# Start of an attention backward kernel reordered, 32 matmuls put ahead of it, and all wq and wo loads tied to program order two ticks earlier

## The chip, the cores and the metric

The kernel runs on one core of one Trainium2 chip. A core has a matrix engine (PE, whose weight loads are listed apart as PEld), a vector engine (DVE), a scalar engine (ACT), a GpSimd engine (POOL) and a sync engine (SP). The engines run side by side, each through its own list of instructions in order, and wait for each other through semaphores. Transfers are issued by SP and by POOL in this kernel and are carried out by 16 DMA engines that both share. The metric is the device time of one execution in microseconds (us), as the median of several runs.

## The reference

Two independent attention blocks, A and B, are computed forward and backward. For each block

```python
q = (x @ wq).reshape(B, Sq, H, Dh).transpose(0, 2, 1, 3)
scores = einsum("bhqd,bhkd->bhqk", q, k_cache) * Dh ** -0.5
p = softmax(scores)
o = einsum("bhqk,bhkd->bhqd", p, v_cache)
out = o.transpose(0, 2, 1, 3).reshape(B, Sq, H * Dh) @ wo
```

with B = 8 batches, Sq = 96 queries, D = 640, H = 32 heads, Sk = 512 keys and Dh = 128, all in bfloat16. The two outputs are concatenated. Results are this output and, for a given `grad_out`, the gradients of x, k_cache, v_cache, wq and wo of both blocks. So each of the 2 x 32 x 8 = 512 pairs of a head and a batch needs the scores, the softmax P, the output O, and backward dV = P^T dO, dP = dO V^T, dS = P (dP - row sum of O dO), dK = dS^T Q and dQ = dS K; around these stand the projections of each head (Q = x wq, dO = g wo^T) and the weight gradients (dwo = O^T g, dwq = x^T dQ).

## The kernel before, in words

The program is written as many small closures. Each is entered in a list with a tick and a slot (`Emitter.add`), the list is sorted by tick, then slot, and the closures are called in that order. One tick is one pair of a head and a batch; head h of a block begins at `c0t = tick0 + 8 h`, and block B follows block A without a pause. The table `OFF` says how many ticks after its own tick a stage of a pair runs: the scores S and the exponential at +3, the normalised P at +3, the transpose of P and dV at +4, O at +5, dP and dS at +6, dK at +7, dQ at +8. So one tick holds stages of several pairs, and the matrix engine's list interleaves them.

The table `HK` does the same for the work of a whole head: `pA` (line 172) loads wo of the head and, on even heads, wq of two heads; `pB` (line 186) transposes both on PE; `pC` (line 207) computes QT (which = 0) and dOT (which = 1), each in a piece of 512 and one of 256 columns; `pD` (line 227) transposes them to dOnat and Qnat; `qA`, `qB`, `qD` make dwo and dwq. After the last head of a group of five or six heads, `gU` (line 488) sums the group's part of the output and of dx, spread over the following ticks.

For one pair: SP loads K and V of two batches at a time. K is transposed either on PE (`c_s1`, line 260, with the copy KT_pe by DVE) or by a DMA transpose, V always by a DMA transpose VT (`c_xt`). PE makes S (line 278); DVE takes the negative row maximum `negm` (280); ACT makes the exponential E_sb (290); DVE takes the reciprocal `rinv` (300); POOL multiplies to P_sb (309); PE transposes P (332) and makes dV (349), O (325), dP (377), and so on. POOL also multiplies O by dO (`prod`, 367), and it issues the stores of dV and dK (358), the stores of dwo (461), dwq (483) and the first block's output (513), and all loads of wo and wq (179, 180) but the first wq.

The tile framework places instructions on each engine's list by its own planning, which may differ from the order of the calls; an instruction that has gone through `keep_in_program_order` (`pinned`, line 107) keeps its place between the neighbours that it was written with. In the kernel before, `pA` of block A pins the loads of heads 1 to 8, and the rest are placed by the planner. wo_h has nine buffers, wq_p two. A buffer of wo_h comes free when `gU` of its group has read it.

The start of block A: SP's first transfers are the first four sixths of x, wq of heads 0 and 1, the rest of x, K, g (the block's half of grad_out, in two parts), V, and more K and V. PE transposes x (six pieces of five 128x128 transposes, `setup_T`, line 118), each piece copied to xT by DVE, then wo and wq of head 0, then g, each piece copied to gT by ACT; then come QT, dOT, dOnat, Qnat and the first scores. For block B the same x and g pieces are loaded into `ld_tmp` by POOL (line 114) and transposed during the last ticks of block A.

Of the kernel before, what the change touches and what calls it, by code (L numbers as in the profile page):

```python
# [10 lines left out]
F32 = mybir.dt.float32  # L11
BF16 = mybir.dt.bfloat16
# [28 lines left out]
SL_HEAD = 90  # L41
SL_GRP = 95
SL_SETUP = 96

OFF = dict(ldk=-5, ldv=-3, kt=-1, vt=2, s2=3, s3=3, s4=4, s5=5, s6=6, s7=7, s8=8)
HK = dict(pA=-7, pB=-3, pC0=[-2, 0], pC1=[-1, 0], pD1=1, pD0=2, qA0=13, qA1=17, qB=[20, 17], qD=[(18, 0, 2), (19, 2, 4), (20, 4, 5)])
EV = dict(pB0="act", pB1="dve", pC00="act", pC01="act", pC10="act", pC11="dve", pD0="dve", pD1="dve", qA0="dve", qA1="dve", qB0="act", qB1="act", qD="dve", gU="act")
GSPREAD0 = 9
PRIO_OFF = 2000
# [4 lines left out]
def build_block(tc, em, tick0, blk, x, kc, vc, wq, wo, g_all, out_all, dx, dk, dv, dwq, dwo, ident, ones, pools, HG=6, first=True, groups=None):  # L54
    nc = tc.nc
    B, Sq, D = x.shape
    _, H, Sk, Dh = kc.shape
# [6 lines left out]
    NB = 2  # L64
    assert B % NB == 0 and H % 2 == 0
    scale = float(Dh) ** -0.5
    HG = min(HG, H)
# [26 lines left out]
    const, ps, kvp, wk, hd, hst, grp = (pools[k] for k in ("const", "ps", "kvp", "wk", "hd", "hst", "grp"))  # L94

    def bank(shape, dt, name):
        return ps.tile(shape, dt, name=name, tag="bank")
# [20 lines left out]
    def setup_T(which_, t):  # L118
        def f():
            key = "xT" if which_ == 0 else "gT"  # L120
            if t == 0:
                S[key] = const.tile([128, DC, T], BF16, name=key, bufs=1)
            dst = S[key]
            if first:
                tmp = S["x_nat" if which_ == 0 else "g_nat"][:, t, :]
            else:
                tmp = S.pop(("tmp", which_, t))
            pt = bank([128, DC * 128], BF16, "tp_ps")
            for c in range(DC):
                nc.tensor.transpose(pt[:, c * 128:(c + 1) * 128], tmp[:, c * 128:(c + 1) * 128], ident[:])  # L130
            evac("act" if first and which_ == 1 else "dve", dst[:, :, t * 128:(t + 1) * 128], pt[:].rearrange("p (c k) -> p c k", k=128))
        return f

    def setup_nat(which_):
# [20 lines left out]
    def evac(eng, dst, src, sc=None):  # L155
        if eng == "act":
            nc.scalar.activation(dst, src, ACT.Identity, scale=(1.0 if sc is None else sc))
        else:
            if sc is None:
                nc.vector.tensor_copy(dst, src)  # L160
            else:
                nc.vector.tensor_scalar(dst, src, float(sc), None, op0=ALU.mult)

    xg = [(0, t) for t in range(min(4, TT))] + [(1, t) for t in range(min(4, TT))] + [(w, t) for w in (0, 1) for t in range(4, TT)]
    for i, (which_, t) in enumerate(xg):
        if not first:
            em.add(tick0 - 12 + i // 2, SL_LOAD, setup_ld(which_, t))
        em.add(tick0 + ((-8 if which_ == 0 else -3) if first else -8 + i // 2), SL_SETUP, setup_T(which_, t))
    em.add(tick0 + (-11 if first else B + OFF["s5"] - 2), SL_LOAD + 1, setup_nat(1))
    em.add(tick0 + (-12 if first else B + OFF["s8"] - 2), SL_LOAD, setup_nat(0))  # L170

    def pA(h):
        def f():
            wo_h = hst.tile([128, D], BF16, name="wo_h", bufs=HG + 3)
            order = pinned if first and 0 < h < HG + 3 else (lambda ins: ins)
            if h % 2 == 0:
                wq_p = hd.tile([128, DC, 256], BF16, name="wq_p", bufs=2)
                with nc.allow_non_contiguous_dma(reason="wq slice of two heads"):
                    order((nc.sync if first and h == 0 else nc.gpsimd).dma_start(wq_p[:], wq_v[:, :, h * 128:(h + 2) * 128]))
            order(nc.gpsimd.dma_start(wo_h[:], wo[h * 128:(h + 1) * 128, :]))  # L180
            if h % 2 == 1:
                wq_p = HS[(blk, h - 1)]["wq_p"]
            HS[(blk, h)] = dict(wo_h=wo_h, wq_p=wq_p, wq_h=wq_p[:, :, (h % 2) * 128:(h % 2 + 1) * 128])
        return f
# [329 lines left out]
        return f  # L514

    NTS = len(tsplits)
    S45 = pools["S45"]
    S78 = pools["S78"]
    for g in range(NG):
        h0 = GH0[g]  # L520
        for hh in range(groups[g]):
            h = h0 + hh
            c0t = tick0 + h * B
            if not (first and h == 0):
                em.add(c0t + HK["pA"], SL_LOAD, pA(h))
            em.add(c0t + HK["pB"], SL_HEAD, pB(h))
            for si in range(NTS):
                em.add(c0t + HK["pC0"][min(si, len(HK["pC0"]) - 1)], SL_HEAD, pC(h, 0, si))
                em.add(c0t + HK["pC1"][min(si, len(HK["pC1"]) - 1)], SL_HEAD, pC(h, 1, si))
            em.add(c0t + HK["pD1"], SL_HEAD, pD(h, 1))  # L530
            em.add(c0t + HK["pD0"], SL_HEAD, pD(h, 0))
            for b in range(B):
                ct = c0t + b
                if b % NB == 0:
                    em.add(tick0 - 12 if first and h == 0 and b == 0 else ct + OFF["ldk"], SLOTS["LOAD"], c_ld(h, b, "K", 7))
                    em.add(ct + OFF["ldv"], SLOTS["LOAD"], c_ld(h, b, "V", 5))
                    if (b // NB) % 2 == 1:
                        em.add(ct + OFF["kt"], SLOTS["LOAD"] + 1, c_xt(h, b, "KT", 2))
                    em.add(ct + OFF["vt"], SLOTS["LOAD"] + 1, c_xt(h, b, "VT", 3))
                if (b // NB) % 2 == 0:  # L540
                    em.add(ct + 2, SLOTS["S1"], c_s1(h, b))
                em.add(ct + OFF["s2"], SLOTS["S2A"], c_s2a(h, b))
                em.add(ct + OFF["s2"], SLOTS["S2B"], c_s2b(h, b))
                em.add(ct + OFF["s3"], SLOTS["S3A"], c_s3a(h, b))
                em.add(ct + OFF["s3"], SLOTS["S3B"], c_s3b(h, b))
                em.add(ct + OFF["s5"], SLOTS["S5B"], c_s5b(h, b))
                if b % 2 == 1:
                    em.add(ct + OFF["s4"] + 1, SLOTS["LOAD"], c_st(h, b, "v"))
                    em.add(ct + OFF["s7"] + 1, SLOTS["LOAD"], c_st(h, b, "k"))
                em.add(ct + OFF["s4"], SLOTS["S4"], c_s4(h, b))  # L550
                S45.setdefault(ct + OFF["s5"], [None, None, None])[0] = (blk, h, b)
                S45.setdefault(ct + OFF["s4"], [None, None, None])[1] = (blk, h, b)
                S45.setdefault(ct + OFF["s6"], [None, None, None])[2] = (blk, h, b)
                S78.setdefault(ct + OFF["s8"], [None, None])[0] = (blk, h, b)
                S78.setdefault(ct + OFF["s7"], [None, None])[1] = (blk, h, b)
                em.add(ct + OFF["s6"], SLOTS["S6"], c_s6(h, b))
                em.add(ct + OFF["s7"], SLOTS["S7"], c_s7(h, b))
            em.add(c0t + HK["qA0"], SL_HEAD, qA(h, 0))
            for di in range(len(dsplits)):
                em.add(c0t + HK["qB"][min(di, len(HK["qB"]) - 1)], SL_HEAD + 1, qB(h, di))  # L560
            em.add(c0t + HK["qA1"], SL_HEAD, qA(h, 1))
            qd_parts = HK["qD"]
            for (k_, c_lo, c_hi) in qd_parts:
                if c_lo < DC and h % 2 == 1:
                    em.add(c0t + k_, SL_HEAD + 2, qD(h, c_lo, min(c_hi, DC)))
        cLg = tick0 + (h0 + groups[g] - 1) * B + B - 1
        gs0 = max(3, (GSPREAD0 * groups[g]) // HG)
        gs1 = max(3, (GSPREAD1 * groups[g]) // HG)
        if g == 0:
            em.add(cLg + OFF["s5"] - 2, SL_LOAD, setup_acc)  # L570
        subs = [(0, t, gi) for t in range(TT) for gi in range(len(gsplits))] + [(1, t, gi) for t in range(TT) for gi in range(len(gsplits))]
        n_out = TT * len(gsplits)
        for i, (which, t, gi) in enumerate(subs):
            if which == 0:
                tk = cLg + OFF["s5"] + 2 + (i * gs0) // n_out
            else:
                tk = cLg + OFF["s8"] + 2 + gs0 - 3 + ((i - n_out) * gs1) // n_out
            em.add(tk, SL_GRP, gU(g, which, t, gi))
# [5 lines left out]
def _kernel_impl(tc, A_x, A_k_cache, A_v_cache, A_wq, A_wo, B_x, B_k_cache, B_v_cache, B_wq, B_wo, grad_out,  # L584
           out_0, out_1, out_2, out_3, out_4, out_5, out_6, out_7, out_8, out_9, out_10, HG=6, slots=None, off=None, hk=None, ev=None, gspread=None, groupsA=None, groupsB=None):
    global GSPREAD0, GSPREAD1
    nc = tc.nc
# [10 lines left out]
    with ExitStack() as ctx:  # L598
        P = lambda **kw: ctx.enter_context(tc.tile_pool(**kw))
        cst = P(name="gconst", bufs=1)  # L600
        ident = cst.tile([128, 128], BF16, name="ident")
        make_identity(nc, ident[:])
        ones = cst.tile([128, 1], BF16, name="ones")
        nc.vector.memset(ones[:], 1.0)
        pools = dict(
            const=P(name="const", bufs=1),
            ps=P(name="ps", bufs=8, space=PSUM),
# [4 lines left out]
            grp=P(name="grp", bufs=1),  # L612
            stp=P(name="stp", bufs=6),
        )
        pools["S45"] = {}
        pools["S78"] = {}
        pools["HS"] = {}
        pools["CS"] = {}
        em = Emitter()
# [78 lines left out]
```

## Time and profile before

| what | value |
|---|---|
| median of 7 runs | 1749.64 us (1746.97 to 1758.2) |
| the profiled execution | 1751.22 us, its span 1749.1 us |
| PE busy | 1679.8 us, 96% |
| PE weight loads busy | 1328.8 us, 76% |
| ACT busy | 1415.6 us, 81% |
| DVE busy | 1334.0 us, 76% |
| POOL busy | 1049.2 us, 60% |
| data moved | 424.69 MB, mean 243 GB/s |

The span reaches from the first to the last instruction of the profiled execution, and its own time is 2.1 us longer. An engine's busy time is the union of its instructions' times. A row of a group of instructions names the line, the engine, the operation and its output and inputs, then the count, the busy time, the mean of one in ns, and the idle time of the engine just before, with what ended it. A row of the timeline has the start, the duration from the first start to the last end, the instruction, a count for merged neighbours, and in brackets the idle time before it and its releaser. In a row of the stretches the granted clock of PE comes after the engines' busy times, then the share of the DMA engines' time taken by packets (it can exceed 1, as packets of several queues overlap) and the rate.

### The profile page before, as it was taken

How to read it: one execution, taken by the hardware profiler on the slowest of the kernel's cores; microseconds unless marked ns; L12 is line 12 of the kernel's file. 1: busy time of each engine (PE TensorE's matmuls, PEld its weight loads, DVE VectorE, ACT ScalarE, POOL GpSimd, SP SyncE). 2: the span in 40 equal slices, each digit the busy share in tenths (PEclk: the TensorE clock that was granted, in tenths of full speed). 3: DMA queues.
4: the chain of work that ended last, by engine and by line, in shares of the span. 5: the costliest groups of instructions: out<-in, count | busy, mean ns of one | idle time of the engine just before them, and what ended most of it. 6: DMA issues, size and time to landing. Idle time of an engine off the chain costs nothing.

```text
span 1749.1 us, 57509 instructions
## 1 busy us (share of the span) xinstructions
PE 1679.8 (96%) x21730; PEld 1328.8 (76%) x21944; DVE 1334.0 (76%) x3043; ACT 1415.6 (81%) x4023; POOL 1049.2 (60%) x1759
## 2 busy tenths in 40 slices
PE   7999999999999999999898999999999999999998
PEld 6777778777778778777677777787787787787785
DVE  5777578778788788787677876787788787788785
ACT  6888789878879869878667997897797797798793
POOL 3666556656656656657466665665565665565563
PEclk9999999999999999999999999999999999999999
DMA  9999999999999989989999999999999899999893
GB/s 231 249 246 278 244 234 267 261 225 234 264 222 258 269 211 264 264 222 231 230 261 257 263 277 229 232 271 241 220 254 251 222 274 244 213 274 249 200 257 123
DMA packets 603751, 424.69 MB, mean 243 GB/s; under 512 B 425633, under 2 KB 560417, under 8 KB 603473
## 3 DMA queue, kind: packets, MB, share of 16 engines
q1 hardware_dynamic: 548752, 239.22, 69.1%
q0 software_dynamic: 54720, 181.78, 32.3%
q8 instruction: 172, 2.82, 0.7%
q14 instruction: 107, 0.87, 0.2%
HBM read 161.09 MB, written 159.12 MB: 183 GB/s over the span
## 4 chain that ended last, share of the span: by engine, by line
PE 72%; DVE 9%; ACT 7%; DMA 7%; issue 4%; POOL 2%; SPq 0%; ACTq 0%; POOLq 0%; DVEq 0%
PE o_ps L498 11%; PE q_ps L223 11%; PE dwo_ps L457 5%; PE dwq_ps L477 5%; PE S_ps L278 5%; PE dK_ps L419 5%; PE dV_ps L349 5%; PE dP_ps L377 5%; PE dq_dst_ps L402 4%; PE optp_ps L332 4%; PE optp_ps L325 4%; PE dq_dst_ps L395 3%; DVE negm L280 3%; ACT E_sb L290 3%; DVE dS_sb L381 3%
## 5 line engine op out<-in xcount | busy, mean ns | idle before, releaser
L309 POOL TENSOR_SCALAR P_sb<-E_sb,rinv 96x512 bf16<-96x512 bf16 x512 | 350.8, 685 | 409.1 <-DVE rinv L300 405.8
L290 ACT ACTIVATE E_sb<-S_ps,negm 96x512 bf16<-96x512 f32 x512 | 349.1, 682 | 195.8 <-DVE negm L280 189.8
L381 DVE SCALAR_TENSOR_TENSOR dS_sb<-dP_ps,dl_ps,P_sb 96x512 bf16<-96x512 f32 x512 | 383.0, 748 | 99.6 <-PE dl_ps L379 70.9
L280 DVE TENSOR_REDUCE negm<-S_ps 96x1 f32<-96x512 f32 x512 | 347.5, 679 | 63.1 <-PE S_ps L278 58.3
L422 ACT ACTIVATE dK_sb<-dK_ps 128x512 bf16<-128x512 f32 x512 | 301.3, 588 | 57.5 <-PE dK_ps L419 37.8
L352 ACT ACTIVATE dV_sb<-dV_ps 128x512 bf16<-128x512 f32 x512 | 313.5, 612 | 11.6 <-DMA out_dram<-dV_sb 10.1
L358 POOL DMA_DIRECT2D out_dram<-dV_sb x256 | 194.8, 761 | 130.4 <-ACT dV_sb L352 89.6
L338 ACT ACTIVATE PT_sb<-optp_ps 128x384 bf16<-128x384 bf16 x512 | 254.5, 497 | 1.4 <-PE optp_ps L332 1.4
L358 POOL DMA_DIRECT2D out_dram<-dK_sb x256 | 192.3, 751 | 38.5 <-ACT dK_sb L422 28.4
L367 POOL TENSOR_TENSOR prod<-OT_h,dOT_h 128x96 bf16<-128x96 bf16 x512 | 186.0, 363 | 44.5 <-ACT OT_h L335 36.3
L377 PE MATMUL dP_ps<-VT,dOT_h 128*96 128x512 bf16 x512 | 195.5, 382 | 9.4 <-DMA VT<-V_sb 9.0
L349 PE MATMUL dV_ps<-dOnat_h,P_sb 96*128 96x128 bf16 x2048 | 198.4, 219 | 1.1 <-ACT dV_sb L352 1.0
L419 PE MATMUL dK_ps<-Qnat_h,dS_sb 96*128 96x128 bf16 x2048 | 198.1, 219 | 0.0
L404 DVE COPY dST_sb<-dq_dst_ps 128x384 bf16<-128x384 bf16 x512 | 176.4, 345 | 24.0 <-PE dq_dst_ps L402 23.9
L402 PE MATMUL dq_dst_ps<-ident,dS_sb 96*128 96x96 bf16 x2048 | 172.5, 206 | 11.9 <-DVE dS_sb L381 11.9
L332 PE MATMUL optp_ps<-ident,P_sb 96*128 96x96 bf16 x2048 | 171.9, 205 | 7.2 <-POOL P_sb L309 6.8
L325 PE MATMUL optp_ps<-PT_sb,V_sb 128*128 128x96 bf16 x2048 | 172.4, 206 | 2.7 <-ACT dV_sb L352 2.5
L395 PE MATMUL dq_dst_ps<-dST_sb,K_sb 128*128 128x96 bf16 x2048 | 170.8, 206 | 0.0
L395 PEld LDWEIGHTS <-K_sb 128*128 128x128 bf16 x2048 | 132.0, 98 | 29.6 <-issue 5.7
L300 DVE RECIPROCAL rinv<-rowsum 96x1 f32<-96x1 f32 x512 | 80.2, 157 | 92.5 <-ACT E_sb L290 83.2
L223 PE MATMUL q_ps<-gT,woT_h 128*128 128x512 bf16 (+1 forms) x625 | 136.4, 324 | 0.8
L457 PE MATMUL dwo_ps<-g_nat,Onat 128*128 128x128 bf16 (+1 forms) x708 | 130.2, 295 | 3.4 <-issue 0.2
(84 smaller groups left out, 3789.5 us busy)
## 6 DMA issues: line engine op xcount, KB each, us to landing
out_dram<-dV_sb POOLq DMA_DIRECT2D x256, 256.0 KB, 4.7
out_dram<-dK_sb POOLq DMA_DIRECT2D x256, 256.0 KB, 4.7
K_sb<-in_A_k_cache_dram SPq DMA_DIRECT2D x128, 256.0 KB, 4.6
V_sb<-in_A_v_cache_dram SPq DMA_DIRECT2D x128, 256.0 KB, 4.8
K_sb<-in_B_k_cache_dram SPq DMA_DIRECT2D x128, 256.0 KB, 4.5
V_sb<-in_B_v_cache_dram SPq DMA_DIRECT2D x128, 256.0 KB, 4.6
out_dram<-dwo_sb POOLq DMA_DIRECT2D x64, 160.0 KB, 4.4
out_dram<-dwq_sb POOLq DMA_DIRECT2D x32, 320.0 KB, 4.8
```

Of the source, the lines that this page charges most:

```text
L223: nc.tensor.matmul(q_ps[:], lhs(c), rhsT[:, c, t0:t0 + w], start=(c == 0), stop=(c == DC - 1))
L280: nc.vector.tensor_reduce(negm[:], S_ps[:], axis=AX.X, op=ALU.max, negate=True)
L290: nc.scalar.activation(E_sb[:], st["S_ps"][:], ACT.Exp, bias=st["negm"][:], scale=1.0, accum_out=rowsum[:])
L309: nc.gpsimd.tensor_scalar(P_sb[:], st["E_sb"][:], st["rinv"][:], 0.0, op0=ALU.mult, op1=ALU.add)
L349: nc.tensor.matmul(dV_ps[:, c * 128:(c + 1) * 128], P_sb[:, c * 128:(c + 1) * 128], hs["dOnat_h"][:, b * 128:(b + 1) * 128], start=True, s ...
L352: nc.scalar.activation(SB[(blk, h, b // 2, "v")][:, b % 2], dV_ps[:], ACT.Identity, scale=1.0)
L358: nc.gpsimd.dma_start(dst[b - 1:b + 1, h].rearrange("b (p c) d -> p b (c d)", c=KC), SB.pop((blk, h, b // 2, which))[:])
L377: nc.tensor.matmul(dP_ps[:], hs["dOT_h"][:, tok], st["VT"], start=True, stop=True)
L381: nc.vector.scalar_tensor_tensor(dS_sb[:], dP_ps[:], dl_ps[:, 0:1], st["P_sb"][:], op0=ALU.subtract, op1=ALU.mult)
L395: nc.tensor.matmul(dQT_ps, st["K_sb"][:, c, :], st["dST_sb"][:, c * Sq:(c + 1) * Sq], start=(c == 0), stop=(c == KC - 1))
L419: nc.tensor.matmul(dK_ps[:, c * 128:(c + 1) * 128], dS_sb[:, c * 128:(c + 1) * 128], hs["Qnat_h"][:, b * 128:(b + 1) * 128], start=True, s ...
L422: nc.scalar.activation(SB[(blk, h, b // 2, "k")][:, b % 2], dK_ps[:], ACT.Identity, scale=1.0)
```

## The change

- The table entry `pA` moves from -7 to -9, so the loads of wq and wo stand two ticks earlier in the program, and all of them but those of block A's head 0 are pinned to program order, in both blocks.
- For block A, the six transposes of g move from tick -3 to tick +3, and of head 0 the two pieces of dOT to tick 3 and dOnat to tick 3, Qnat to tick 4, all behind the first scores.
- The copies to xT and gT of block A go to ACT for even pieces and to DVE for odd ones, where DVE had all of xT and ACT all of gT.
- A 128x128 tile of ones is set by DVE, and 32 matmuls of it by itself into one PSUM bank stand first on PE's list. Nothing reads their result.
- The condition for transposing K on PE is moved into a function with the same value.

```diff
-HK = dict(pA=-7, pB=-3, ...
+HK = dict(pA=-9, pB=-3, ...
...
-            evac("act" if first and which_ == 1 else "dve", dst[:, :, t * 128:(t + 1) * 128], pt[:].rearrange("p (c k) -> p c k", k=128))
+            evac("act" if first and t % 2 == 0 else "dve", dst[:, :, t * 128:(t + 1) * 128], pt[:].rearrange("p (c k) -> p c k", k=128))
...
-        em.add(tick0 + ((-8 if which_ == 0 else -3) if first else -8 + i // 2), SL_SETUP, setup_T(which_, t))
+        em.add(tick0 + ((-8 if which_ == 0 else 3) if first else -8 + i // 2), SL_SETUP, setup_T(which_, t))
...
-            order = pinned if first and 0 < h < HG + 3 else (lambda ins: ins)
+            order = (lambda ins: ins) if first and h == 0 else pinned
...
+            fh = first and h == 0
             for si in range(NTS):
                 em.add(c0t + HK["pC0"][min(si, len(HK["pC0"]) - 1)], SL_HEAD, pC(h, 0, si))
-                em.add(c0t + HK["pC1"][min(si, len(HK["pC1"]) - 1)], SL_HEAD, pC(h, 1, si))
-            em.add(c0t + HK["pD1"], SL_HEAD, pD(h, 1))
-            em.add(c0t + HK["pD0"], SL_HEAD, pD(h, 0))
+                em.add(c0t + (3 if fh else HK["pC1"][min(si, len(HK["pC1"]) - 1)]), SL_HEAD + (7 if fh else 0), pC(h, 1, si))
+            em.add(c0t + (3 if fh else HK["pD1"]), SL_HEAD + (8 if fh else 0), pD(h, 1))
+            em.add(c0t + (4 if fh else HK["pD0"]), SL_HEAD, pD(h, 0))
...
+        warm = cst.tile([128, 128], BF16, name="warm")
+        nc.vector.memset(warm[:], 1.0)
...
+        warm_ps = pools["ps"].tile([128, 128], F32, name="warm_ps", tag="bank")
+        for _ in range(32):
+            nc.tensor.matmul(warm_ps[:], warm[:], warm[:], start=True, stop=True)
```

More of the change, by code (lines that the diff above doesn't have):

```diff
@@ L45 @@
 OFF = dict(ldk=-5, ldv=-3, kt=-1, vt=2, s2=3, s3=3, s4=4, s5=5, s6=6, s7=7, s8=8)
-HK = dict(pA=-7, pB=-3, pC0=[-2, 0], pC1=[-1, 0], pD1=1, pD0=2, qA0=13, qA1=17, qB=[20, 17], qD=[(18, 0, 2), (19, 2, 4), (20, 4, 5)])
+HK = dict(pA=-9, pB=-3, pC0=[-2, 0], pC1=[-1, 0], pD1=1, pD0=2, qA0=13, qA1=17, qB=[20, 17], qD=[(18, 0, 2), (19, 2, 4), (20, 4, 5)])
 EV = dict(pB0="act", pB1="dve", pC00="act", pC01="act", pC10="act", pC11="dve", pD0="dve", pD1="dve", qA0="dve", qA1="dve", qB0="act", qB1="act", qD="dve", gU="act")
@@ L516, in build_block, with k_on_pe @@
     NTS = len(tsplits)
+    def k_on_pe(h, b):
+        return (b // NB) % 2 == 0
     S45 = pools["S45"]
@@ L536, in build_block @@
                     em.add(ct + OFF["ldv"], SLOTS["LOAD"], c_ld(h, b, "V", 5))
-                    if (b // NB) % 2 == 1:
+                    if not k_on_pe(h, b):
                         em.add(ct + OFF["kt"], SLOTS["LOAD"] + 1, c_xt(h, b, "KT", 2))
                     em.add(ct + OFF["vt"], SLOTS["LOAD"] + 1, c_xt(h, b, "VT", 3))
-                if (b // NB) % 2 == 0:
+                if k_on_pe(h, b):
                     em.add(ct + 2, SLOTS["S1"], c_s1(h, b))
```

## The prediction, written before the result was known

> **What bounds the kernel now.** I read the page first: is one engine full?
>
> ```profile
> span 1749.1 us, 57509 instructions
> PE 1679.8 (96%) x21730; PEld 1328.8 (76%) x21944; DVE 1334.0 (76%) x3043; ACT 1415.6 (81%) x4023; POOL 1049.2 (60%) x1759
> ```
>
> PE is the bound, with 69.3 us idle. So only PE's idle time, and matmuls run at a slow clock, can be won. Next I asked who PE waits for:
>
> ```profile
> PE dq_dst_ps L402 <- DVE dS_sb L381: 11.9, 32, 0.8
> PE dP_ps L377 <- DMA VT<-V_sb: 9.0, 5, 3.6
> PE optp_ps L332 <- POOL P_sb L309: 6.8, 7, 3.6
> PE tp_ps L130 <- DMA x_nat<-in_A_x_dram: 5.4, 2, 5.1
> ```
>
> (total us, times, longest). The same view by stretches puts these waits in two places, the first 150 us and 800 to 930 us (the step from block A to B); from 200 to 800 us PE is busy 196 to 197 of each 200 us. The stretches of the start:
>
> ```profile
> 10.00:15.00 5.00, 4.33 (x34) 3.72 (x36) 0.49 (x1) 3.83 (x7) 0.00 (x0) 1.00 1.10 347
> 15.00:20.00 5.00, 4.05 (x41) 3.06 (x40) 2.55 (x5) 1.99 (x5) 0.00 (x0) 1.00 1.14 187
> 20.00:25.00 5.00, 2.54 (x28) 1.78 (x28) 2.24 (x7) 3.32 (x11) 1.70 (x3) 0.93 1.14 276
> 25.00:30.00 5.00, 4.95 (x50) 3.87 (x49) 3.31 (x8) 3.60 (x9) 2.54 (x5) 0.73 0.85 191
> 30.00:35.00 5.00, 5.00 (x66) 3.90 (x63) 3.65 (x9) 5.00 (x15) 3.12 (x5) 1.00 0.62 145
> ```
>
> PE (first busy figure) stands half idle from 20 to 25 us, and the clock falls to 0.73 just after. The timeline says why:
>
> ```profile
> 10.61 3.38 PE L130 MATMUL tp_ps<-ident,g_nat 128*128 128x128 bf16 x30 [0.63 <-DMA g_nat<-in_grad_out_dram]
> 18.39 0.38 PE L278 MATMUL S_ps<-KT_pe,QT_h 128*96 128x512 bf16 x1
> 20.53 0.38 PE L278 MATMUL S_ps<-KT_pe,QT_h 128*96 128x512 bf16 x1 [1.48 <-DVE KT_pe L267]
> 20.66 0.68 POOL L309 TENSOR_SCALAR P_sb<-E_sb,rinv 96x512 bf16<-96x512 bf16 x1 [17.72 <-DVE rinv L300]
> 23.96 0.34 PE L332 MATMUL optp_ps<-ident,P_sb 96*128 96x96 bf16 x4 [1.31 <-POOL P_sb L309]
> ```
>
> The first S comes at 18.39, after g, dO and most of the natural transposes, which do not need it; then PE has nothing left to cover the softmax chain S, negm, E, rinv, P (2.3 us from S to P). Idle from 18.9 to 23.96: 3.3 us.
>
> **What the Trainium skill says.** "TensorE: Matmul & The Clock Gate", Part 1: PE starts at half clock, is freed after about one sustained busy window of 3.4 us, free-running, and falls back after an idle one; a 128-column matmul starts every 107 ns cold and 56 ns warm. The trace agrees: 30 transposes of g take 3.38 us (113 ns each) at 10.61, while five matmuls of 512 columns take 1.24 us at 15.00, and the clock shows 3.4 us steps at half (0.73 above). "DMA: Bandwidth & Descriptors", Issuing engines are not separate DMA queues: all issuers share 16 engines. The trace agrees: in crowded stretches (share above 1) POOL's loads land late, up to 14.1 us.
>
> **The change, part by part**, against the profiled 1751.22 us.
>
> *Warm-up.* 32 x 107 ns (the skill's cold price; the trace's 113 gives 3.6) = 3.4 us, from about 1.0 us, when DVE's ones are set (its memset of 128x1 ends at 0.87; the wide one I put at 0.1 us). They end near 4.5, and PE idles to 5.05 anyway for x: cost 0. If that cover went, x would be late by up to 0.5 us. What it wins is uncertain: 3.4 us just fills one window, at an unknown phase. If it fails, x (30 transposes) stays cold, as now.
>
> *Scores ahead of g.* x's last piece lands at 7.62, so warmth buys nothing before that. Then, warm, by the trace's warm steps (58 ns per transpose, 0.22 us per 512 columns): 10 transposes 0.6, wo and wq 0.6, QT 1.6 us: 10.5. The x copies, now on ACT (0.72) and DVE (0.49), keep up; ACT does the last of its three by 8.7, then woT_h and QT by 11. K landed at 8.76, KT_pe is ready at about 11.2, the first S at 11.3 against 18.39. Its chain of 2.3 us plus the gT copies queued before it on ACT (0.7) gives P at about 14.5 against 20.66. PE meanwhile has g (1.7), dOT (1.6) and dOnat (0.45), so dO is late next: dOnat's copy ends near 18.3, held by three gT copies on each of ACT and DVE and by negm of the second pair on DVE. The second P comes at about 19.3 against 23.21, and PE starts wo of head 1 near 20.0 against 24.41: 4.4 us. Without warmth QT costs 1.6 us more, and the gain is about 3. On top, the clock step at half after 24.3 us (3.4 us at half, 1.7 us lost) comes from the idle stretch that goes: 0 to 1.7. What may cut this is transfer: the DMA share is 1.10 to 1.14 from 10 to 25 us, falls to 0.85, 0.62 and 0.92 from 25 to 40 us, and is 1.11 to 1.15 from 40 to 200. Against 1.14 the slack of 25 to 40 us is 1.3 + 2.3 + 1.0 = 4.6 us; a faster start can use up no more. SP's K, V and transposes keep their order. I take 4.5, from 2.5 to 6.
>
> *Loads in program order.* The loads number the same. The planned lists show the move: before, POOL issues five or six wo loads in a burst when a group ends; after, one each 8 ticks, wq each 16. In quiet stretches bursts cost little (the whole of 200 to 800 us has 3 to 4 us idle per 200). One is different:
>
> ```profile
> 919.58 0.72 POOL L358 DMA_DIRECT2D out_dram<-dV_sb  x1 [0.65 <-DMA x_nat<-in_B_x_dram]
> 921.76 0.54 POOL L180 DMA_DIRECT2D wo_h<-in_B_wo_dram  x1 [0.91 <-DMA out_dram<-dV_sb]
> 923.55 0.55 POOL L513 DMA_DIRECT2D out_dram<-ob  x1 [1.25 <-DMA out_dram<-dK_sb]
> 925.35 0.72 POOL L358 DMA_DIRECT2D out_dram<-dK_sb  x1 [1.26 <-DMA wo_h<-in_B_wo_dram]
> 926.44 1.35 POOL L309 TENSOR_SCALAR P_sb<-E_sb,rinv 96x512 bf16<-96x512 bf16 x2
> 927.19 0.34 PE L332 MATMUL optp_ps<-ident,P_sb 96*128 96x96 bf16 x4 [3.57 <-POOL P_sb L309]
> ```
>
> POOL's transfers reuse eight semaphores in turn, so each issue waits for the eighth before it. Five wo loads among the crowded stores fill the eight; P_sb is queued behind, and PE stands 3.57 us. After, one wo load stands there: the four loads less are 4 x 0.55 = 2.2 us of issue and their 4.1 us of waits. P should come by 920 to 921, ahead of PE's need at 923.6. Gain 3.6, from 0 to 4.
>
> The price is paid at 820 to 855 us: wo of B's heads 0 to 3 and wq of 0 and 1 land by 775 now, and after are issued from about 823 on, wo of head 0 and 1 being additional there (wq takes the place of another wq). Two loads of 160 KB at the 225 GB/s of 840 to 860 us are 1.4 us of transfer; the grad pieces go ahead of wq, which may save part of PE's 1.88 us wait for them. Net -1 to +2; I take 0.6 lost. Early in block A, wq and wo of heads 2 and 3 move ahead of the fourth and fifth P on POOL (0.91 + 0.57 us), where PE has QT of head 1 to do: 0, at most 1.
>
> *The rest*: ordinary bursts 0.3 won; the copied condition 0.
>
> Sum: -4.5 - 3.6 + 0.6 - 0.3 = -7.8, so 1743.4 for the profiled execution. That lies 1.6 us over the median, so 1741.8 against 1749.64; as gains of this sort are partly given back at the next transfer, I say **1742.5 us**.
>
> **Rivals.** *Half comes back* (1746.5): transfers bind from 40 to 200 us, where VT already makes PE wait 3.2 us, so 3 to 4 us of the start turn into longer VT waits. For: shares of 1.11 to 1.15. Against: the slack of 4.6 us. *More is won* (1736.5): besides, the half-clock step at 48.2 us (1.7 us after 1.4 us idle) and the one at 843.5 (behind a 3.60 us wait for VT) go, with 2 to 3 us of idle. They hang on small idle times that any shift moves. *Nothing is moved* (1749): PE's early work is only reshuffled, and another POOL transfer holds P at 920. *Slower* (1756): wq and wo of B's head 0 come too late. They are issued at about 825; PE needs them at 849.16, and works in order, so every us of lateness beyond that counts, with 1.7 more for the clock. The longest landing in the trace, 14.1 us, leaves 10 us. It decides from a landing of 24 us on; to eat 7 us of gain and end 6 us above takes about 36.
>
> **How the numbers follow.** Both gains about as summed 0.50; half comes back 0.22; more 0.13; nothing 0.07; slower 0.08. About 0.3% (5.25 us, so 1744.4) is what a measurement can tell from no change. Of the first case 0.43 lies below 1744.4, of the second 0.08, with 0.13 of the third: faster 0.64. Same: 0.07 + 0.14 + 0.07 = 0.28. Slower 0.08. The range 1736 to 1750 leaves out the slower case and part of the third; the likeliest alone is 1738.5 to 1746.
>
> **What would show it.** S at 11 to 12 us (13 to 14 if cold); x transposes at 58 ns if the warm-up worked; wo of head 1 at 19 to 21.5; no clock step at 24; waits for VT up to 150 us near 3 us still; the 3.57 us wait for P near 927 gone; wo of B's head 0 landed before its transposes. It would be wrong if PE's idle from 25 to 200 us grew by what the start saves, or if 815 to 880 us lost 4 us more than its present 10.8 (54.2 of 65 us busy).

## The result, and the profile after

The change makes the kernel slower. Its median is 1760.27 us (25 runs), against 1746.8 us (62 runs) for the kernel before: ratio 1.0083, 95% interval 1.0062 to 1.0104, or about 14 us. 1742.5 us with a range of 1736 to 1750 was forecast. Single runs of a kernel spread over some 30 us; the medians here are over all runs, and the ratios leave out those that lie over 1.5% above the fastest of the same kernel, so a ratio is not quite the quotient of two medians.

The first thing to see is that the two profiled executions do not show it. The page of the changed kernel opens:

```profile
span 1750.0 us, 57499 instructions
PE 1682.4 (96%) x21761; PEld 1329.5 (76%) x21976; DVE 1334.4 (76%) x3044; ACT 1415.2 (81%) x4023; POOL 1052.0 (60%) x1759
```

The profiled execution took 1751.73 us, against 1751.22 us before: 0.5 us apart, where the medians are 13.5 us apart. The changed kernel's profile is 8.5 us below its own median, and that of the kernel before 4.4 us above the median of its 62 runs. So a subtraction of these two profiles cannot give the effect. They still serve for two things: what happens in the order of events, and where one execution loses a lead that it had.

**The start went as meant.** The timeline of the first 22 us, after (start, duration, instruction, and in brackets PE's or POOL's idle time and its releaser):

```profile
1.09 3.60 PE L624 MATMUL warm_ps<-warm 128*128 128x128 bf16 x32 [1.09 <-DVE warm L611]
5.07 1.29 PE L130 MATMUL tp_ps<-ident,x_nat 128*128 128x128 bf16 x20 [0.38 <-DMA x_nat<-in_A_x_dram]
7.90 1.14 PE L130 MATMUL tp_ps<-ident,x_nat 128*128 128x128 bf16 x10 [1.54 <-DMA x_nat<-in_A_x_dram]
13.21 0.38 PE L278 MATMUL S_ps<-KT_pe,QT_h 128*96 128x512 bf16 x1 [0.52 <-DVE KT_pe L267]
15.79 0.68 POOL L309 TENSOR_SCALAR P_sb<-E_sb,rinv 96x512 bf16<-96x512 bf16 x1 [12.85 <-DVE rinv L300]
```

The first S comes at 13.21 (18.39 before), the first P at 15.79 (20.66). The 20 transposes of x run warm, at 65 ns each; the last ten take 114 ns each, as PE was at half clock again from 8.06 us on. It had just waited 1.54 us for x's second part. The stretches of the start, after:

```profile
10.00:15.00 5.00, 4.26 (x44) 3.08 (x44) 2.29 (x6) 2.12 (x5) 0.00 (x0) 0.85 1.11 349
20.00:25.00 5.00, 4.35 (x58) 3.35 (x59) 3.61 (x8) 4.49 (x14) 2.85 (x6) 1.00 1.14 261
25.00:30.00 5.00, 4.70 (x62) 3.44 (x61) 3.37 (x9) 4.34 (x12) 3.93 (x6) 1.00 0.99 268
```

From 20 to 30 us PE is busy 9.05 us, against 7.49 before, and the clock stays at 1.00 where it stood at 0.93 and 0.73.

**The lead is then lost again.** I compared the start of P on POOL pair by pair, after minus before: -4.9 us at the first pair, -12.4 us at the 61st, -10.1 us at the 161st, -8 us at the 251st to 271st, -4.0 us at the 311th, -1.7 us at the 511th. The loss is spread over the whole length. The stretches of the two long quiet parts say the same; before:

```profile
200.00:790.00 590.00, 580.63 (x7538) 459.31 (x7615) 463.09 (x1058) 487.18 (x1388) 360.59 (x603) 1.00 1.02 245
1000.00:1690.00 690.00, 676.82 (x8825) 536.41 (x8913) 538.59 (x1231) 575.36 (x1641) 418.29 (x700) 1.00 1.03 244
```

and after:

```profile
200.00:790.00 590.00, 577.23 (x7471) 455.98 (x7548) 460.82 (x1054) 482.63 (x1376) 355.96 (x594) 1.00 1.02 241
1000.00:1690.00 690.00, 673.50 (x8731) 532.12 (x8819) 533.64 (x1217) 570.91 (x1627) 417.56 (x696) 1.00 1.04 244
```

PE's idle time in these 1280 us grows from 22.6 to 29.3 us, and it gets through 16367 weight loads (the counts behind PEld) instead of 16528: 1.0% less of the program, or 12.5 us. Every engine's count falls: the whole pipeline is held up, at the same clock and nearly the same DMA share. (PE's idle time is an upper bound here: both traces lack 214 and 215 matmul records out of some 21950 that the weight loads account for.) PE's own list of waits changes little. A change that can be seen is in ACT's waits for transfers. Before:

```profile
ACT dV_sb L352 <- DMA out_dram<-dV_sb: 10.1, 6, 2.5
ACT dK_sb L422 <- DMA out_dram<-dK_sb: 2.8, 2, 2.2
```

and after:

```profile
ACT dV_sb L352 <- DMA out_dram<-dV_sb: 17.1, 13, 3.4
ACT dK_sb L422 <- DMA out_dram<-dK_sb: 13.9, 12, 2.8
```

That is 31.0 us in 25 waits instead of 12.9 us in 8. ACT wants to write a dV or dK tile whose last store hasn't left. These waits are not the measure of the loss, though: a kernel below that isn't slower (*start only*) has 21.0 us in 13 of them, and the slowest of all (*extra loads in dense ticks*) only 15.9 us in 15. One such stall in a quiet part, after:

```profile
454.57 0.60 ACT L352 ACTIVATE dV_sb<-dV_ps 128x512 bf16<-128x512 f32 x1 [1.73 <-DMA out_dram<-dV_sb]
455.21 0.33 PE L325 MATMUL optp_ps<-PT_sb,V_sb 128*128 128x96 bf16 x4 [0.62 <-ACT dV_sb L352]
```

A late store holds ACT 1.73 us, and PE 0.62 us behind it. In the step from A to B, finally, P still arrives late, by 2.63 us instead of 3.57, though only one wo load stands there:

```profile
907.55 0.57 POOL L180 DMA_DIRECT2D wo_h<-in_B_wo_dram  x1 [0.24 <-DMA g_nat<-in_grad_out_dram]
916.06 0.71 POOL L358 DMA_DIRECT2D out_dram<-dK_sb  x1 [3.42 <-DMA x_nat<-in_B_x_dram]
917.89 0.34 PE L332 MATMUL optp_ps<-ident,P_sb 96*128 96x96 bf16 x4 [2.63 <-POOL P_sb L309]
```

**A pattern in the ticks.** In the ticks in which `gU` sums a group's output and dx, PE has more work: before, such a tick takes 3.92 us, any other 2.94 us. I call them sum ticks and dense ticks; each has about the same stores, K, V and VT to move, so the dense ones have the least time for them. Counted by POOL's issues in the two profiles, the planner of the kernel before puts 56 of the 64 wo loads into sum ticks, since these free the buffers; after, one load each eight ticks, only 26 are there. Of the 31 wq loads on POOL it is 11 before and 15 after. So 30 wo loads move from ticks with more work for PE into ticks with less. The landing times follow (mean us from issue to landing, before to after; over 232 dense and 146 sum ticks of the quiet parts): in dense ticks VT 5.53 to 6.69, dK store 4.79 to 5.61, dV store 4.81 to 5.60, B's K 4.56 to 5.53; in sum ticks VT 5.07 to 5.05, dK store 4.33 to 4.06. The mean dense tick grows from 2.938 to 2.989 us, the mean sum tick goes from 3.919 to 3.912: 232 x 0.051 = 11.8 us. This is a reading of two profiles, to be tested; the same sum scatters by about 5 us between profiles, and in one kernel below (the last of the table) it is as high as after without a slower median.

The landing times hold up better when all thirteen profiles of this document are counted in the same way. In dense ticks VT lands in a mean of 5.5 to 6.0 us in the nine kernels that aren't measurably slower than the one before (itself among them), and in 6.5 to 6.7 us in the four that are. This goes with the loss; it doesn't show through which waits PE loses the time.

### The profile page after: what moved, and what is told of

Read it like the earlier page. It is cut to its first block, busy times and chain, and to the rows that moved or that the text cites. A ratio compares the mean times of both kernels' runs of the same rounds, so it can differ in the third digit from the quotient of the medians.

```text
span 1750.0 us, 57499 instructions
## 1 busy us (share of the span) xinstructions
PE 1682.4 (96%) x21761; PEld 1329.5 (76%) x21976; DVE 1334.4 (76%) x3044; ACT 1415.2 (81%) x4023; POOL 1052.0 (60%) x1759
## 4 chain that ended last, share of the span: by engine, by line
PE 66%; DMA 11%; DVE 9%; ACT 8%; issue 4%; POOL 2%; ACTq 0%; SPq 0%; POOLq 0%; DVEq 0%
PE o_ps L498 11%; PE q_ps L223 10%; DMA out_dram<-dK_sb 5%; PE dwo_ps L457 4%; PE S_ps L278 4%; PE dwq_ps L477 4%; PE dV_ps L349 4%; PE dK_ps L419 4%; PE dP_ps L377 4%; PE dq_dst_ps L402 3%; PE optp_ps L325 3%; PE optp_ps L332 3%; PE dq_dst_ps L395 3%; DMA out_dram<-dV_sb 3%; ACT E_sb L290 3%
## 5 line engine op out<-in xcount | busy, mean ns | idle before, releaser
L223 PE MATMUL q_ps<-gT,woT_h 128*128 128x256 bf16 (+1 forms) x624 | 136.8, 325 | 1.5 <-ACT gT L157 0.6
```

What stands on the lines that cost most here:

```text
L223: nc.tensor.matmul(q_ps[:], lhs(c), rhsT[:, c, t0:t0 + w], start=(c == 0), stop=(c == DC - 1))
```

## The experiments

Two theories stood against each other. *Start*: the early start is worth nothing, or does harm later. *Loads*: the loads, spread and tied to program order, cost more than the start wins; and if so by being pinned, by being two ticks earlier, or by the bytes they add to dense ticks. All results in one table; each ratio of an experiment is to runs of the kernel before on the same chip, and the kernels were spread over several chips:

| kernel | median us | ratio [95%] |
|---|---|---|
| the change | 1760.27 | 1.0083 [1.0062, 1.0104] |
| start only | 1743.99 | 0.9994 [0.9974, 1.0014] |
| loads only | 1757.73 | 1.0051 [1.0029, 1.0073] |
| start, loads pinned at -7 | 1751.04 | 1.0037 [1.0013, 1.0062] |
| the same, wo into sum ticks | 1745.56 | 0.9990 [0.9965, 1.0015] |
| before + 52 extra loads, dense ticks | 1763.34 | 1.0108 [1.0072, 1.0143] |
| before + 52 extra loads, sum ticks | 1744.06 | 0.9981 [0.9950, 1.0013] |
| before + 52 small extra loads, dense ticks | 1747.95 | 1.0017 [0.9994, 1.0040] |
| start only, 1 warm-up matmul | 1741.77 | 0.9986 [0.9962, 1.0010] |
| wo and wq into sum ticks | 1746.11 | 0.9998 [0.9965, 1.0031] |
| the change (-9), wo into sum ticks | 1746.93 | 0.9999 [0.9973, 1.0026] |
| wo into sum ticks but at the step | 1747.81 | 1.0015 [0.9985, 1.0046] |

### The two halves of the change

**Start only**: the change with the loads as before.

```diff
-HK = dict(pA=-9, ...
+HK = dict(pA=-7, ...
-            order = (lambda ins: ins) if first and h == 0 else pinned
+            order = pinned if first and 0 < h < HG + 3 else (lambda ins: ins)
```

> The whole change but its loads: pA stays at -7 and only heads 1 to 8 of block A are pinned, so 56 of 64 wo loads fall into ticks that also hold group sums, as before. Theory 1 (the start wins about 12 us, and wo loads moved into ticks without sums lose it and more): ratio to before 0.993 to 0.996, 7 to 12 us faster. Rival (transfers bind overall, so a lead at the start is given back later whatever the loads do): ratio 0.998 to 1.003.

Measured 0.9994 [0.9974, 1.0014]: no loss, so the loss of the change is not in the start. The gain expected from the profile is missed too, though the events came as meant; the ratio lies where the rival had it. Its timeline:

```profile
5.22 2.07 PE L130 MATMUL tp_ps<-ident,x_nat 128*128 128x128 bf16 x20 [0.53 <-DMA x_nat<-in_A_x_dram]
11.64 0.38 PE L278 MATMUL S_ps<-KT_pe,QT_h 128*96 128x512 bf16 x1 [0.52 <-DVE KT_pe L267]
```

Here S comes at 11.64. The later kernels tell how much lead there is. The 41st P starts at a mean of 135.4 us in five profiles with the old start (before 141.05, loads only 133.73, the three with extra loads 132.51, 136.91 and 132.74) and at 130.9 us in the eight with the new one: 4.5 us, or 3.1 us without the profile of before. They also show that the profile of before had an unlucky start: its first S came at 18.39, the other four's at 16.7 to 17.0 us. Of the 12 us lead that the two first profiles showed at the 61st pair, much was that.

**Loads only**: the reverse of that edit, made in the kernel before.

```diff
-HK = dict(pA=-7, ...
+HK = dict(pA=-9, ...
-            order = pinned if first and 0 < h < HG + 3 else (lambda ins: ins)
+            order = (lambda ins: ins) if first and h == 0 else pinned
```

> The kernel before with only the loads of the change (pA at -9, all pinned but head 0 of block A): 26 of 64 wo loads are left in ticks with sums. Theory 1: slower by 14 to 26 us, ratio 1.008 to 1.015, with ticks outside the sums longer by 0.05 us or more and ticks with sums unchanged. Rival (the lead at the start is given back): ratio 0.998 to 1.003.

Measured 1.0051 [1.0029, 1.0073], so the loads alone make it slower, if less than expected. Nothing else moved: PE's weight loads, the lists of ACT, DVE and SP, and POOL's list without its wq and wo loads are in the same order, instruction by instruction, in the traces of this kernel and of the one before. (The same holds for the change and *start only*.) So the loss can't come from other work that the planner rearranged. The ACT waits for stores, 31.1 us in 19, are as in the change:

```profile
ACT dK_sb L422 <- DMA out_dram<-dK_sb: 16.6, 9, 3.3
ACT dV_sb L352 <- DMA out_dram<-dV_sb: 14.5, 10, 3.5
```

### Pinned, two ticks earlier, or in the wrong ticks?

**Pinned at -7**: the change, with `pA` back at -7 but all loads still pinned.

```diff
-HK = dict(pA=-9, ...
+HK = dict(pA=-7, ...
```

> The change with pA left at -7 and all loads pinned: 22 of 64 wo loads in ticks with sums. Theory 1: as slow as the change, ratio 1.005 to 1.012. Rival (it is the two ticks, which bring a load beside other transfers): as fast as the start alone, 0.993 to 0.997.

Measured 1.0037 [1.0013, 1.0062]: slower without the two ticks, by less than expected of the spreading. Here 22 of the 64 wo loads stand in sum ticks. The interval just touches that of the change (1.0062 to 1.0104), but the loads alone, at -9, gave 1.0051 between the two; whether the two ticks add to the cost of spread loads isn't settled.

**wo into sum ticks**: all loads pinned as in the last one, with wo from the tenth load on entered by hand, one per tick, behind the output sums of the group whose buffer it takes.

```diff
+    def wo_tick(h):
+        j = blk * H + h - (HG + 3)
+        jb, jh = j // H, j % H
+        gj = max(i for i in range(NG) if GH0[i] <= jh)
+        cl = tick0 - (blk - jb) * H * B + (GH0[gj] + groups[gj]) * B - 1
+        return cl + OFF["s5"] + 2 + max(3, (GSPREAD0 * groups[gj]) // HG) + jh - GH0[gj]
...
+            if blk * H + h >= HG + 3:
+                em.add(wo_tick(h), SL_LOAD, pW(h))
```

> The start of the change, all loads pinned, wq at -7, but each wo load from the tenth on put by hand one to a tick behind the output sums of the group whose buffer it takes over, so 56 of 64 lie in ticks with sums again. Theory 1: as fast as the start alone, 0.993 to 0.997. Rival (pinning itself, a load that holds POOL's list, is what costs): as slow as the change, 1.005 to 1.012.

Measured 0.9990 [0.9965, 1.0015]: the loss is gone, though the gain that was expected besides (0.993 to 0.997) isn't there. So it isn't the pinning. 56 wo loads stand in sum ticks, as the planner had them.

**The change, wo into sum ticks**: the same edit with `pA` at -9.

> The change with pA at -9 and all loads pinned, but wo loads from the tenth on put into ticks with sums: 56 of 64 again, wq 15 of 31. Theory 1 alone (two ticks cost only through wo loads in ticks without sums): as e4_wo_in_sums, 0.996 to 1.001. Rival (two ticks cost by themselves, the 0.5% between the change and its pinning at -7): 1.003 to 1.006.

Measured 0.9999 [0.9973, 1.0026]. This is the change with nothing altered but where wo stands (wq at -9 stays), and 0.8% is gone. With wo in sum ticks, two ticks more lead cost nothing that can be measured.

### What a load costs in each kind of tick

Three kernels add 52 loads to the kernel before: values of wo, 128x640 each time (160 KB) in the first two and 128x64 (16 KB) in the third, go to a scratch tile that nothing reads.

**Extra loads in dense ticks**:

```diff
+    def pX(h):
+        def f():
+            x_d = stp.tile([128, 640], BF16, name="x_dum", bufs=1)
+            pinned(nc.gpsimd.dma_start(x_d[:], wo[h * 128:(h + 1) * 128, 0:640]))
+        return f
...
+            if g > 0:
+                em.add(tick0 + h0 * B + 24 + 4 * hh, SL_LOAD, pX(h))
```

> The kernel before with 52 extra loads of a head's wo (160 KB each) into a scratch tile that nothing reads, pinned one each four ticks in ticks that hold no group sums. Theory 1 (bytes in ticks without sums cost, at 0.2 to 0.5 us for each 160 KB): 11 to 26 us slower, ratio 1.006 to 1.015. Rival (the order of the real loads matters, not the bytes): 0.998 to 1.003.

Measured 1.0108 [1.0072, 1.0143]: 18.8 us for 52 loads, 0.36 us each (0.24 to 0.48 by the interval). Its ACT waits for stores are near those of before, 15.9 us against 12.9:

```profile
ACT dV_sb L358 <- DMA out_dram<-dV_sb: 8.1, 8, 2.4
ACT dK_sb L428 <- DMA out_dram<-dK_sb: 7.8, 7, 2.6
```

So late stores in front of ACT are one way in which the delay shows, and not the only one; through which waits these 18.8 us pass isn't shown.

**Extra loads in sum ticks**: the same, at `7 + 2 * hh` in place of `24 + 4 * hh`.

> The same 52 extra loads of 160 KB, pinned one each two ticks in ticks that hold group sums. Theory 1: hidden, ratio 0.999 to 1.003. Rival (bytes or POOL's issue time cost wherever they stand): as the extra loads in the other ticks, 1.006 to 1.015.

Measured 0.9981 [0.9950, 1.0013]: free, with the same bytes and the same number of issues on POOL. The two sets differ in more than the kind of tick, as they stand two ticks apart here and four there; but the real loads, moved from dense ticks to sum ticks one to a tick, agree. Its ACT waits and quiet stretches:

```profile
ACT dV_sb L358 <- DMA out_dram<-dV_sb: 4.1, 4, 1.6
ACT dK_sb L428 <- DMA out_dram<-dK_sb: 2.3, 3, 1.3
```

```profile
200.00:790.00 590.00, 581.27 (x7574) 456.50 (x7571) 461.08 (x1054) 484.07 (x1379) 371.39 (x623) 1.00 1.06 251
1000.00:1690.00 690.00, 682.01 (x8904) 536.09 (x8902) 538.52 (x1229) 575.90 (x1642) 432.60 (x726) 1.00 1.06 251
```

The DMA share is 1.06, above the 1.02 and 1.04 of the change, which loses. So the mean share over a long stretch doesn't say whether transfers bind.

**Small extra loads in dense ticks**: the places of the first, with 64 of the 640 columns (16 KB).

> 52 extra loads at the places of the first of these, but of 64 of the 640 columns (16 KB each): the same number of issues on POOL and of turns of the eight semaphores, a tenth of the bytes. Theory 1 (bytes): ratio 0.999 to 1.004. Rival (POOL's issue time of about 0.55 us, or the semaphores): as the full loads, 1.006 to 1.015.

Measured 1.0017 [0.9994, 1.0040]. With a tenth of the bytes at the same places, most of the loss is gone. An issue takes POOL as long as before (0.60 us in the mean for both sizes); so it is the bytes (with the time in which they are moved), and not POOL's issues or its turns of semaphores.

### The parts that were to win

**Start only with 1 warm-up matmul** in place of 32:

```diff
-        for _ in range(32):
+        for _ in range(1):
```

> The start alone, with 1 instead of 32 matmuls ahead of it. If the warm-up does what the prediction took: x's transposes cold at 113 ns, the first scores 1 to 3 us later, ratio to before 0.0005 to 0.002 above the start alone (0.9994), thus 1.000 to 1.0015. Rival (the warm-up does not reach the scores): as the start alone.

Measured 0.9986 [0.9962, 1.0010], not told apart from 0.9994 with 32; the small loss expected isn't seen. Its timeline:

```profile
12.73 0.38 PE L278 MATMUL S_ps<-KT_pe,QT_h 128*96 128x512 bf16 x1 [0.52 <-DVE KT_pe L267]
```

S is 1.1 us later than in the start-only kernel (x's first 20 transposes take 2.31 us, 116 ns each), and no time is lost for it that the runs can show.

**wo into sum ticks but at the step**: wo of B's heads 4 to 8, five loads that stand together near 920 us, spread at -7.

```diff
+        if H - groups[-1] <= j < H:
+            return tick0 + h * B + HK["pA"]
```

> As e4_wo_in_sums, but the five wo loads of block B's heads 4 to 8 stay at -7, one each eight ticks, so that they no longer stand together among the crowded transfers of the step from block A to B. If the wait for P near 920 us (6.51 us in the profile of e4_wo_in_sums, none with the loads alone) is a standing cost of the burst: the wait is gone and the ratio to before is 0.994 to 0.997, below that of e4_wo_in_sums. Rival (what is won there is spent at the next crowded transfer): wait gone, ratio 0.998 to 1.001.

Measured 1.0015 [0.9985, 1.0046]; nothing won, which is the rival's case. In the kernel with all in sum ticks, PE waits 6.51 us for P there, in the start-only kernel 7.99:

```profile
918.32 0.50 PE L332 MATMUL optp_ps<-ident,P_sb 96*128 96x96 bf16 x4 [7.99 <-POOL P_sb L309]
```

The wait is a standing one: the nine profiles with the five loads together have 2.7 to 8.0 us of it, the four with them spread none or, after the change, 2.63. With the five spread in this kernel there is no such wait for P; from 880 to 940 us this one stands in the waits of PE:

```profile
PE dV_ps L366 <- ACT dV_sb L369: 3.3, 1, 3.3
```

**wo and wq into sum ticks**: wq too goes to the last sum tick of the 15 ticks up to 7 before its head, where there is one; 21 of the 31 are then in sum ticks, with 56 of wo.

```diff
-                em.add(c0t + HK["pA"], SL_LOAD, pA(h))
+                em.add(wq_tick(h), SL_LOAD, pA(h))
```

> The start of the change, wo loads in ticks with sums as in e4_wo_in_sums, and each wq load from block A's head 8 on put into the last tick with sums among the 15 ticks up to seven before its head, where there is one: 21 of 31 wq loads now lie in such ticks, 11 before. Theory 1 at the dose measured (18.8 us for 52 loads of 160 KB, 0.36 us each): ten loads of 320 KB less in the other ticks, 7 us less than e4_wo_in_sums, ratio to before 0.993 to 0.997. Rival (the dose holds for extra loads only, and moving real ones wins nothing): 0.998 to 1.001.

Measured 0.9998 [0.9965, 1.0031], the expected gain is missed. Taking still more loads out of dense ticks wins nothing. The loss per load is thus not a fixed price: bytes added to the dense ticks of the kernel before cost time, bytes taken from them win none. That this kernel lay just on the good side of the point from which transfers bind would fit, and isn't shown. None of these kernels is faster than the one before beyond the interval.

## Why the prediction was wrong, step by step

- **Warm-up, priced at 0 and of uncertain gain: right.** It costs nothing (x at 5.07, as foretold) and wins nothing that the median shows. In the changed kernel's profile the clock even fell back at half from 8.1 to 11.5 us, and S came at 13.21, the "13 to 14 if cold" of the list; in the start-only profile at 11.64, near the 11.3. That the phase is unknown came true: after the same 32 matmuls, full clock began at 4.65 us in the one and at 6.90 us in the other, where most of x's first 20 transposes were still cold.
- **Scores ahead of g, -4.5 us: the mechanism was right, and so was the size in the profiles.** The 41st P is 3.1 to 4.5 us earlier in the mean, inside the 2.5 to 6 given, and none of the eight profiles with the new start has the clock step near 20 to 24 us that all five with the old one have. In the median it comes to -1.0 us (-4.5 to +2.4 by the interval of 0.9994). Where the rest goes isn't settled: single profiles scatter by about 5 us, as much as the term. In the start-only profile 4.4 us of it could be in the wait for P at 918 us, 7.99 us instead of 3.57.
- **The burst at 915 to 927 us, -3.6 us: right in the cause, wrong in what it is worth.** Spread, the wait shrinks to 2.63 us in the change, but with the wait gone altogether nothing was won (the last row of the table); in that profile a late store stopped PE instead.
- **The step from A to B, +0.6 us: nothing speaks against it.** PE is busy 57.16 of the 65 us from 815 to 880, where it was 54.20. The rival *slower* named late weights of B's head 0: its wo landed at 831.22 and PE needed it at 841.0. The kernel did get slower, but not by this.
- **Ordinary bursts, 0.3 us won: this is the step that failed.** It looked at what bursts cost where they stand, saw "3 to 4 us idle per 200", and put the loads' new places at nothing. The sum never asked what a load costs there. The runs show that the planner's bursts stood where loads are free, and that spread loads cost: the loads alone make the kernel before slower by 0.51%, some 9 us (5 to 13), and putting wo back into sum ticks takes the whole loss of the change away (0.9999). The extra loads give an estimate of the missing term: 30 wo loads x 0.36 us = 10.8 us.
- **What stays open: the size.** Against the start-only kernel, 1.0083 / 0.9994 = 1.0089 says about 15.5 us (10 to 21) for the same loads that cost some 9 us by themselves; the ranges overlap. Nor does the count of loads settle it: pinned at -7, 34 wo loads are moved into dense ticks, and the loss is 0.37%, some 6.5 us, where 34 x 0.36 would be 12. In the two profiles with wo spread at -9, ACT waits much for dK's stores (13.9 us after, 16.6 us with loads only); pinned at -7, little:

```profile
ACT dK_sb L422 <- DMA out_dram<-dK_sb: 2.0, 2, 1.6
```

  Whether the place at -9 is the worse one, no run isolates. The clock may have a part: the mean granted clock over all runs is 0.9934 for the change and 0.9946 before, which makes (0.0066 x 1760) - (0.0054 x 1747) = 2.2 us, and it may follow from the added idle time rather than cause any.
- **The rivals.** *Half comes back* had the right resource, transfers, but the wrong place (40 to 200 us, where the lead still grew to the 61st pair) and too small a loss. *Slower* had 0.08. What was lacking is a rival for the loads in the quiet parts.
- **The base.** The sum was made against a profile whose own start was late by 1.5 us at the first S and 4 us at the 13th P against the others of the same start. One profile cannot show that. The 69.3 us of idle time are too many as well, as 214 matmul records are lacking in that trace. And the 14.1 us that it calls the longest landing in the trace is the longest of POOL's transfers; SP's in the same trace land up to 21.9 us after their issue.

The Trainium skill's "DMA: Bandwidth & Descriptors", Issuing engines are not separate DMA queues, was cited for the crowded stretches alone. Its sentence that all issuers share the 16 engines fits the quiet ones too: with 30 of POOL's loads more in dense ticks, SP's VT lands 1.2 us later there in the mean (5.53 to 6.69).

## What to carry to other kernels

When a load is moved, price its new place and not only the old one: ask how long the step is there, and what else is in transfer. Here, with PE 98% busy and a mean DMA share of 1.02 to 1.06, the same bytes were free in steps of 3.92 us and not in steps of 2.94; a burst in a step with more compute can then be a better place than an even spread. And time both kernels before explaining a difference: two single profiles here hid one of 13.5 us.

## What the runs showed of the hardware that was not expected

- The same 52 loads of 160 KB cost 0.36 us each in ticks of 2.94 us and nothing (-0.19%, -0.50 to +0.13) in ticks of 3.92 us, at nearly the same DMA share in the quiet parts (1.03 and 1.05, 1.06 and 1.06).
- 32 matmuls in 3.60 us didn't always hold the clock. Full clock began at 4.65 us in the changed kernel's profile and at 6.90 us in that of *start only*, though the matmuls (1.09 to 4.69 us) and x's landings (5.02 and 7.86, 5.18 and 7.95) were nearly the same. In the first, the next 3.41 us held both waits for x (0.38 and 1.54 us), PE was busy for the other 1.49, and the 3.41 us after that ran at half clock. In the second they held only the second wait (0.70 us), PE was busy for 2.71, and the clock stayed.
- In all thirteen profiles, the 3.41 us before each step at half clock have PE busy for 0 to 2.02 us. So the clock also fell back after stretches that were far from idle, where the prediction had it fall after an idle one.
- A first S that is some 5 us earlier (11.2 to 13.2 in the eight profiles with the new start, 16.7 to 18.4 in the five with the old) moved the median of 1747 us by -0.06% (-0.26 to +0.14).
